# Another order of the pieces, and of every engine's instructions, in an attention and MLP kernel on one core

## The chip, the core and the metric

The kernel runs on one core of a Trainium2 chip. A core has five engines that run beside each other, each with its own list of instructions that it takes in order: TensorE (PE, matmuls; its weight loads are shown as PEld), VectorE (DVE), ScalarE (ACT), GpSimd (POOL, here mostly an issuer of DMAs) and SyncE (SP, an issuer of DMAs). TensorE writes to PSUM, and VectorE and ScalarE take the results from there. Engines wait for each other through semaphores. The metric is the device time of one execution in microseconds; the median of several runs is given.

## What is computed

A recurrent attention over 768 steps for 4 x 8 heads of 40 features, and a two-layer MLP over the 3072 resulting rows.

```python
for t in range(S):
    y[:, :, t] = np.einsum('bhd,bhde->bhe', rt, state)
    Sa = np.einsum('bhde,bhe->bhd', state, at)
    state_decay = state * wt[:, :, None, :] - np.einsum('bhd,bhe->bhde', Sa, bt)
    state = state_decay + np.einsum('bhd,bhe->bhde', vt, kt)
...
h = x @ w_in
sp = np.where(h > 20.0, h, np.log1p(np.exp(np.minimum(h, 20.0))))
g = h * np.tanh(sp)
return (g @ w_out).astype(np.float32)
```

## The kernel before

**Attention.** The 768 steps are cut into 12 chunks of 64. Within a chunk the recurrence is solved with matrices; only a 40 x 40 state per head goes from chunk to chunk. The work is written as small pieces, each named by a letter and by the chunk c and a half (be or g, 0 or 1). Before the state is needed, a chunk goes through: `l` (loads of w, a, b, k by SP), `p` (`scan`, L290 to L305: eight VectorE instructions that make running products of w, each needing the one before but for two), `g` (`gram`, L320: products of a with b and k on TensorE; ScalarE copies them to GP, L321 and L324; VectorE masks a part into HA, L325) and `k` (`natural`, L336 to L351: transposes on TensorE, copied by ScalarE). Two chunks share one inverse of triangular 32 x 32 blocks: `i` (`inverse`, L356 to L368: 65 VectorE instructions, 30 steps of a product L363 and a sum L365, each needing the one before, then the transpose TT, L367, and one more, L368). `m` (`corner`, L377 and L385: 32 x 32 matmuls on TensorE, with copies on ScalarE between), `b` (`blocks`, ScalarE copies, L393) and `t` (`merge`, L404: 64 x 64 matmuls) make of it the chunk's matrix KT.

**State.** For each chunk and half: `V` (ScalarE puts the state beside v, L426), `A` (TensorE, L434, copied to UVT by ScalarE), `T` (transposes of UVT, L442, copied to UVQ by ScalarE, L443), `D` (transposes of the state, L450, copied by ScalarE, L451), `B` (L462 on TensorE into the PSUM tile pq, of which there is one; VectorE masks it into UVQ in two instructions, L465), `C` (L484 and L491 on TensorE, into pq too; VectorE adds the state, L494, and scales it, L498; ScalarE copies the result to yev, L496). The new state lets the next chunk's V, A and D start. `v`, `u`, `q` are POOL's loads of VS, UVT and bdr for the next chunk, `o` its store of a chunk's result.

**MLP.** It works on 6 blocks of 512 rows. `x` loads a block, `X` splits it into a high and a low part. For each of 8 slices of the hidden layer, `h` (`mlp1`, L656: 16 matmuls, then the Mish on ScalarE), `H` (`split_g`: ScalarE rounds, L663, VectorE takes the rest, L664) and `y` (`mlp2`, L677 to L679: 24 matmuls); `z` stores. `w0` to `w3` and `W0` to `W7` load the two weight matrices in chunks and convert them from 64-bit floats: ScalarE scales (L561), VectorE assembles in three instructions (L563 to L565), ScalarE rounds (L584) and VectorE takes the rest (L585). w0 to w3 have three chunks of 128 x 512 each. `+p`, `+i`, `+e` and `/p`, `/i`, `/e` open and close pools of SBUF.

**What sets the order.** Two texts. `SEQ` lists the pieces in the order in which they are built, which decides the turns in which buffers are used. `PLAN` lists for each engine, in order, every instruction of every piece: `g4.0*16` stands for the next 16 instructions of piece g4.0 on that engine. `Lanes.order` turns each such list into a chain in which every instruction comes after the one ahead of it:

```python
for t in plan.split():
    k, n = (t.split('*') + ['1'])[:2]
    for _ in range(int(n)):
        i = next(q[k])
        if last is not None:
            self.tc.add_manual_dep(i, last.name, info, reason='plan')
        last = i
```

So an engine that waits for one instruction holds back all that stand behind it in its list.

Of the kernel before, what the change touches and what calls it, by code (L numbers as in the profile page):

```python
# [48 lines left out]
    D3.1 B3.0 V3.1 T3.0 l7.1 C3.0 g7.0 A3.1 p7.1 v4 D4.0 V4.0 B3.1 T3.1 k7.0 u4 l8.0 C3.1 q4 g7.1 k7.1 b2 p8.0 D4.1 V4.1
    i3 m2.1 l8.1 m2.0 o3 p8.1 t5.0 t4.0 t4.1 t5.1 A4.1 A4.0 B4.1 v5 g8.0 T4.0 B4.0 C4.0 g8.1 T4.1 C4.1 k8.0 u5 V5.0 l9.0  # L50
    k8.1 D5.0 q5 A5.0 V5.1 o4 D5.1 p9.0 T5.0 l9.1 A5.1 B5.0 T5.1 v6 C5.0 p9.1 g9.0 k9.0 B5.1 u6 l10.0 C5.1 q6 g9.1 V6.0
    k9.1 D6.0 b3 i4 l10.1 m3.1 m3.0 p10.0 D6.1 V6.1 t7.1 t6.0 p10.1 t6.1 g10.0 A6.1 A6.0 o5 B6.1 t7.0 v7 T6.0 B6.0 k10.0
    C6.0 T6.1 l11.0 C6.1 u7 p11.0 V7.0 D7.0 q7 A7.0 g10.1 o6 k10.1 T7.0 B7.0 l11.1 g11.0 C7.0 V7.1 p11.1 D7.1 A7.1 k11.0
    v8 B7.1 T7.1 u8 C7.1 q8 g11.1 V8.0 D8.0 k11.1 /p +p w0 i5 b4 m4.0 V8.1 D8.1 m4.1 o7 t8.1 t8.0 w1 t9.0 A8.1 A8.0 B8.1
    v9 T8.1 t9.1 T8.0 B8.0 C8.0 C8.1 u9 V9.0 D9.0 q9 A9.0 D9.1 V9.1 o8 w2 T9.0 A9.1 B9.0 v10 T9.1 b5 m5.0 C9.0 m5.1 B9.1
    C9.1 D10.0 u10 V10.0 t11.0 q10 t10.0 D10.1 o9 V10.1 t10.1 t11.1 /i +i x0 A10.0 A10.1 B10.0 v11 T10.0 T10.1 C10.0 B10.1
    C10.1 V11.0 D11.0 w3 u11 A11.0 X0 q11 D11.1 V11.1 A11.1 o10 h0.0 x1 B11.0 h0.1 H0.0 C11.0 H0.1 h0.3 B11.1 h0.2 X1
    C11.1 /e +e W0 h0.5 H0.2 H0.3 h0.4 o11 H0.5 x2 h0.6 W1 H0.4 h0.7 W2 y0.0 h1.0 X2 y0.1 H0.7 W3 h1.1 H0.6 x3 y0.2 W4
    h1.2 H1.0 h1.3 y0.3 W5 X3 h1.4 H1.1 y0.4 W6 y0.5 h1.5 W7 y0.6 H1.2 H1.3 h1.6 y0.7 z0.0 z0.1 y1.0 H1.4 h1.7 H1.5 z0.2
    z0.3 h2.1 x4 y1.1 H1.6 y1.2 H1.7 y1.3 H2.1 X4 y1.4 y1.5 h2.0 h2.2 H2.0 y1.6 H2.2 y1.7 h2.3 H2.3 h2.4 z1.0 y2.0 z1.1  # L60
    H2.4 h2.5 z1.2 z1.3 h2.7 H2.5 y2.1 h2.6 y2.2 H2.6 H2.7 y2.3 x5 h3.1 y2.4 H3.1 h3.0 X5 H3.0 y2.5 y2.6 y2.7 h3.2 H3.2
    z2.0 z2.1 h3.3 z2.2 y3.0 h3.5 z2.3 H3.3 h3.4 H3.5 H3.4 y3.1 y3.2 h3.6 H3.6 y3.3 h3.7 h4.2 H3.7 h4.0 H4.2 y3.4 H4.0
    h4.1 y3.5 y3.6 H4.1 y3.7 h4.3 h4.4 H4.3 z3.0 z3.1 H4.4 y4.0 h4.6 z3.2 z3.3 y4.1 h4.5 H4.5 y4.2 y4.3 H4.6 h4.7 y4.4
    H4.7 h5.0 h5.1 H5.0 H5.1 h5.2 y4.5 H5.2 y4.6 h5.3 y4.7 H5.3 z4.0 z4.1 y5.0 h5.4 z4.2 z4.3 H5.4 y5.1 y5.2 h5.5 h5.6
    H5.5 h5.7 H5.6 y5.3 H5.7 y5.4 y5.5 y5.6 y5.7 z5.0 z5.1 z5.2 z5.3
# [8 lines left out]
        D3.0*4 C2.1*32 t3.1*32 g6.1*16 A3.0*16 D3.1*4 k6.1*8 B3.0*32 k6.1*4 T3.0*8 k6.1*4 A3.1*16 C3.0*32 g7.0*16 k7.0*8
        D4.0*4 B3.1*32 T3.1*8 C3.1*16 k7.0*4 C3.1*16 g7.1*16 k7.1*8 D4.1*4 k7.1*4 m2.1*32 k7.1*4 m2.0*32 m2.1*32 m2.0*32
        t5.0*32 t4.0*32 t4.1*32 t5.1*32 A4.1*16 g8.0*16 B4.1*32 A4.0*16 g8.1*16 B4.0*32 T4.0*8 k8.0*12 T4.1*4 C4.0*32 T4.1*4
        D5.0*4 C4.1*32 A5.0*16 k8.1*8 D5.1*4 k8.1*4 T5.0*8 A5.1*16 B5.0*32 g9.0*16 k8.1*4 T5.1*4 C5.0*32 T5.1*4 k9.0*8 B5.1*32
        k9.0*4 C5.1*32 g9.1*16 k9.1*8 D6.0*4 k9.1*4 m3.1*32 k9.1*4 m3.0*32 m3.1*32 D6.1*4 m3.0*32 t7.1*32 t6.0*32 t6.1*32
# [720 lines left out]
```

## Time and profile before

| | us |
|---|---|
| median of 3 runs | 754.79 |
| the 3 runs | 750.35, 757.13, 754.79 |
| the profiled execution | 750.2 |
| its span, from the first to the last instruction | 748.3 |
| first MLP matmul starts | 392.94 |
| last MLP matmul ends | 743.39 |

The columns of a group or timeline line are: start or line, duration, engine, line of the kernel, operation, what is written and read, shape and count; in square brackets, how long the engine stood idle before it and what ended that. A wait line gives the total in us, how many waits and the longest. A window line gives the stretch, its length and the busy time of each engine with the number of its instructions, then the granted share of TensorE's clock. TensorE's matmuls overlap, so that a busy TensorE is not one at its peak. In the trace an ordinary 32-bit matmul has two records; a transpose, or a matmul of the MLP, has one.

### The profile page before, as it was taken

Reading aid. Unit: us, or ns where it says so; the run is one execution under the profiler, and the core shown is the slowest. Engines: PE = TensorE matmul, PEld = TensorE weight load, DVE = VectorE, ACT = ScalarE, POOL = GpSimd, SP = SyncE. Lnnn points to the kernel's source line nnn. Section 1 sums busy time; section 2 is a strip of 40 time slices with the busy share of each in tenths; the row PEclk is TensorE's granted clock in tenths of the full one; section 3 lists DMA queues with packets and bytes.
Section 4 is the critical chain, followed back from the end, with each engine's and each line's share of the span. In section 5 each row is a group of like instructions: output and inputs, shape, how many; then the busy total and the mean of one; then the engine's idle time right before and its main releaser. Section 6 shows DMA issues by size and latency. Waiting matters only on the chain.

```text
span 748.3 us, 22996 instructions
## 1 busy us (share of the span) xinstructions
PE 650.5 (87%) x10184; PEld 581.7 (78%) x10184; DVE 451.2 (60%) x901; ACT 356.6 (48%) x571; POOL 104.1 (14%) x181
## 2 busy tenths in 40 slices
PE   2655688699789799687879999999999999999997
...
DVE  8689979979989979979367777421231121111110
...
PEclk9999999879989889879999999999999999999999
...
GB/s 216 106 94 84 82 31 153 117 57 137 151 39 153 139 37 152 63 77 157 86 195 169 161 167 106 3 117 1 1 120 1 0 36 1 10 27 1 35 1 36
DMA packets 31347, 62.11 MB, mean 83 GB/s; under 512 B 6800, under 2 KB 19216, under 8 KB 31248
## 3 DMA queue, kind: packets, MB, share of 16 engines
...
## 4 chain that ended last, share of the span: by engine, by line
PE 65%; DVE 14%; issue 9%; ACT 5%; DMA 4%; POOL 1%; SPq 0%; ACTq 0%; POOLq 0%; DVEq 0%
PE pa L656 24%; PE pu L679 4%; PE pu L678 4%; PE pu L677 4%; PE pq L679 4%; PE pq L677 4%; PE pq L678 4%; PE pa L404 3%; PE pq L484 2%; PE pq L462 2%; PE pa L320 2%; DVE tmp L363 2%; PE pa L385 2%; DVE XL L365 2%; PE pu L434 2%
## 5 line engine op out<-in xcount | busy, mean ns | idle before, releaser
L664 DVE TENSOR_TENSOR gl<-g,gh 128x1024 fp32r<-128x1024 f32 x48 | 58.7, 1225 | 196.4 <-ACT gh L663 196.2
L656 PE MATMUL pa<-xh,w_ih 128*128 128x512 f32 x288 | 112.9, 392 | 0.0
L656 PE MATMUL pa<-xh,w_il 128*128 128x512 f32 x288 | 96.7, 390 | 0.0
L663 ACT CAST gh<-g 128x1024 fp32r<-128x1024 f32 x48 | 50.1, 1047 | 93.6 <-PE pq L678 93.2
L657 ACT ACTIVATE g<-pa 128x1024 f32<-128x1024 f32 x48 | 49.3, 1026 | 75.4 <-PE pa L656 48.5
L656 PE MATMUL pa<-xl,w_ih 128*128 128x512 f32 x192 | 74.9, 390 | 0.0
L320 PE MATMUL pa<-bk,wa 40*64 40x128 f32 x768 | 35.1, 324 | 33.9 <-DVE bk L303 26.7
L656 PEld LDWEIGHTS pa<-xh,w_il 128*128 128x128 f32 x288 | 54.1, 188 | 11.4
L656 PEld LDWEIGHTS pa<-xh,w_ih 128*128 128x128 f32 x288 | 54.1, 188 | 10.5
L363 DVE TENSOR_TENSOR tmp<-XL 128x30 f32<-128x30 f32 (+9 forms) x180 | 58.6, 326 | 1.6
L365 DVE TENSOR_TENSOR XL<-XL,tmp 128x30 f32<-128x30 f32 (+9 forms) x180 | 58.6, 325 | 1.6
L679 PE MATMUL pq<-w_oh,gl 128*128 128x320 f32 x192 | 59.3, 309 | 0.0
L679 PE MATMUL pu<-w_oh,gl 128*128 128x320 f32 x192 | 59.3, 309 | 0.0
L677 PE MATMUL pq<-w_oh,gh 128*128 128x320 f32 x192 | 59.3, 309 | 0.0
L678 PE MATMUL pq<-w_ol,gh 128*128 128x320 f32 x192 | 59.3, 309 | 0.0
L678 PE MATMUL pu<-w_ol,gh 128*128 128x320 f32 x192 | 59.2, 309 | 0.0
L677 PE MATMUL pu<-w_oh,gh 128*128 128x320 f32 x192 | 59.2, 308 | 0.0
L320 PEld LDWEIGHTS pa<-bk,wa 40*64 40x64 f32 x768 | 28.3, 162 | 37.0 <-DVE bk L303 27.3
L305 POOL DMA_DIRECT2D pD<-P x48 | 35.1, 734 | 122.3 <-DVE w L295 85.6
L484 PE MATMUL pq<-UVQ,bkn 128*64 128x104 f32 (+1 forms) x768 | 41.1, 263 | 11.2 <-DVE UVQ L465 5.1
L484 PEld LDWEIGHTS pq<-UVQ,bkn 128*64 128x64 f32 x768 | 36.5, 144 | 15.4 <-issue 6.8
L465 DVE TENSOR_TENSOR UVQ<-pq,cst 128x512 f32<-128x512 f32 x48 | 32.0, 683 | 18.0 <-PE pq L462 17.8
...
## 6 DMA issues: line engine op xcount, KB each, us to landing
...
```

What stands on the lines that cost most here:

```text
L305: PQ.dma_start(out=pD[c, be, :, al].rearrange("e (s t) -> e s t", t=64), in_=P3[al * 64:al * 64 + 40, :, 0:64])
L320: PE.matmul(pt[o, al, s // 2], a[q, s], bk[q, s], start=(s < 2), stop=True, skip_group_check=True)
L363: V.tensor_tensor(out=tv, in0=X[:, i + 1:32, i:i + 1].broadcast_to([128, 31 - i, i]), in1=X[:, i:i + 1, 0:i].broadcast_to([128, 31 - i, i] ...
L365: V.tensor_tensor(out=X[:, i + 1:32, 0:i], in0=X[:, i + 1:32, 0:i], in1=tv, op=ALU.add)
L484: PE.matmul(py[be * 64:be * 64 + 64, al, s, 0:n], BKN[c, be][:, u * 40:u * 40 + 64], UVQ[be][:, u, 0:n], start=(s == 0), stop=(c == 0), sk ...
L656: PE.matmul(pt[:, j], w, x, start=(n == 0), stop=(n == 7), skip_group_check=True)
L657: A.activation(g, pt, AF.Mish)
L663: A.copy(gh, g)
L664: V.tensor_tensor(out=gl, in0=g, in1=gh.bitcast(F32), op=ALU.subtract)
L677: PE.matmul(po[i][k], gh[:, j, t], oh, start=(f == 0), stop=False, skip_group_check=True)
L678: PE.matmul(po[i][k], gh[:, j, t], ol, start=False, stop=False, skip_group_check=True)
L679: PE.matmul(po[i][k], gl[:, j, t], oh, start=False, stop=(f == 15), skip_group_check=True)
```

## The change

`SEQ` and all five lists of `PLAN` are replaced by others with the same pieces and the same number of instructions of each piece on each engine. No function is changed. What differs, list by list:

- VectorE: more inverse steps stand ahead of the first B mask behind each inverse. Where the list alternated p6.0 with i2 and p10.0 with i4, these p now come in one run ahead of the inverse, and the inverse steps in runs of their own (i2*19, i4*20). w2 is converted ahead of w1. B0.1, B2.1 and B11.1 come ahead of their other halves.
- TensorE: the halves of m and the products of g and k are moved around the state's pieces; C9.0 comes ahead of m5.1, B9.1 ahead of D10.0, T10.1 is cut in two around C10.0. In the MLP, h and y are interleaved differently.
- ScalarE: the copies follow what they serve; behind the second inverse, m1 is served between the copies b1.
- POOL: q0 behind v0, q1 ahead of u1, and a few neighbours swapped.
- SP: w2 ahead of w1, with the last third of w1 behind x0.

```diff
 PLAN = {
     'PE': '''
...
-        k11.0*4 g11.1*16 D8.0*4 k11.1*12 m4.0*32 k11.1*4 D8.1*4 m4.0*32 m4.1*64 t8.1*32 t8.0*32 t9.0*32 A8.1*16 A8.0*16
-        B8.1*32 T8.1*8 t9.1*32 T8.0*4 B8.0*32 T8.0*4 C8.0*32 C8.1*32 D9.0*4 A9.0*16 D9.1*4 T9.0*8 A9.1*16 B9.0*32 T9.1*4
-        m5.0*32 m5.1*32 T9.1*4 C9.0*32 m5.0*32 D10.0*4 B9.1*32 m5.1*32 C9.1*32 t11.0*32 t10.0*32 D10.1*4 t10.1*32 t11.1*32
-        A10.0*16 A10.1*16 B10.0*32 T10.0*8 T10.1*8 C10.0*32 B10.1*32 D11.0*4 A11.0*16 C10.1*32 D11.1*4 A11.1*16 h0.0*16
-        B11.0*32 h0.1*16 C11.0*32 h0.3*16 B11.1*32 h0.2*16 C11.1*32 h0.5*16 h0.4*16 h0.6*16 y0.0*6 h0.7*16 y0.0*18 y0.1*12
...
+        g11.1*16 k11.1*8 D8.0*4 k11.1*4 m4.1*32 k11.1*4 m4.0*32 m4.1*32 D8.1*4 m4.0*32 t9.0*32 t8.1*32 t8.0*32 t9.1*32 A8.1*16
+        A8.0*16 B8.1*32 T8.0*8 T8.1*4 B8.0*32 T8.1*4 C8.0*32 C8.1*32 D9.0*4 A9.0*16 D9.1*4 T9.0*8 A9.1*16 B9.0*32 T9.1*8
+        m5.0*32 C9.0*32 m5.1*32 m5.0*32 B9.1*32 D10.0*4 m5.1*32 C9.1*32 t10.0*32 t11.0*32 D10.1*4 t10.1*32 t11.1*32 A10.0*16
+        A10.1*16 B10.0*32 T10.0*8 T10.1*4 C10.0*32 T10.1*4 B10.1*32 D11.0*4 A11.0*16 C10.1*32 D11.1*4 A11.1*16 h0.0*16
+        B11.1*32 h0.1*16 B11.0*32 h0.3*16 C11.0*32 h0.2*16 C11.1*16 h0.4*16 C11.1*16 h0.5*16 h0.6*16 y0.0*12 h0.7*16 y0.0*12
+        h1.0*16 h1.3*16 h1.1*16 y0.1*15 y0.2*3 y0.1*3 y0.2*3 y0.1*6 y0.2*18 y0.3*12 h1.2*16 y0.3*12 h1.4*16 y0.4*24 h1.5*16
...
     'DVE': '''
...
-        i1 i0 i1*2 p4.0 i1 p4.1 i1 p4.1 i1 p4.1 i1 p4.1 i1 p4.1 i1 p4.1 i1 p4.1 i1 p4.1 i1*12 B0.0 i1 B0.0 i1*4 g4.0 i1*2 C0.0
-        i1 C0.0 i1 C1.0 i1*3 B0.1 i1 B0.1 i1*2 p5.0 i1 p5.0 i1 C0.1 i1 C0.1 i1 p5.0 i1 p5.0 i1 p5.0 i1 p5.0 i1 g4.1 p5.0 i1
-        p5.0 B1.0*2 i1 C1.1 i1*5 g5.0 i1 C1.0 i1 p5.1 i1 p5.1 i1 p5.1 i1 p5.1 i1 p5.1 B1.1*2 p5.1 i1 p5.1 i1 p5.1 i1 C1.0 i1
-        C1.1 i1 g5.1 i2 C1.1 i2 C2.0 i2*2 p6.0 i2 C2.1 i2 p6.0 i2 p6.0 i2 p6.0 i2 p6.0 i2 p6.0 i2 p6.0 i2 p6.0 i2 p6.1 i2 p6.1
-        i2 p6.1 i2 p6.1 i2 p6.1 i2 p6.1 i2 p6.1 i2 p6.1 i2*2 B2.0 i2 B2.0 i2*5 g6.0 i2 C2.0 i2 C2.0 i2 C3.0 i2*3 B2.1 i2 B2.1
...
+        p4.0 i1 p4.0 i1 p4.0 i1 p4.1 i1 p4.1 i1 p4.1 i1 p4.1 i1 p4.1 i1 p4.1 i1 p4.1 i1 p4.1 i1*15 B0.1 i1 B0.1 i1*5 B0.0 i1
+        B0.0 i1 g4.0 i1*3 C0.0 i1 C0.0 i1 C1.0 i1*4 C0.1 i1 C0.1 i1 C1.1 p5.0 i1 p5.0 i1 p5.0 i1 p5.0*3 i1 B1.0*2 p5.0 g4.1
+        p5.0 i1*2 C1.0 i1 p5.1 i1 p5.1 i1 p5.1 i1 g5.0 i1 B1.1 i1 B1.1 i1 p5.1 i1 p5.1 i1 p5.1 C1.0 p5.1 C1.1 p5.1 C1.1 p6.0
+        C2.0 p6.0 C2.1 p6.0*6 i2 g5.1 i2*19 p6.1 i2 p6.1 i2 p6.1 i2 p6.1 i2 p6.1 i2 p6.1 i2 p6.1 i2 p6.1 i2 B2.1 i2 B2.1 i2*3
...
+        i3*2 p9.1 i3 p9.1 B5.1*2 p9.1 i3 p9.1*3 C5.1 p9.1 p10.0 p9.1 C5.1 p10.0 C6.1 p10.0*6 i4 g9.1 i4*20 p10.1 i4 p10.1 i4
...
-        C10.1*2 X0*2 w3*7 B11.0*2 H0.0 w3 H0.1 w3*4 B11.1*2 W0 X1 W0*2 X1*2 W0 H0.2 H0.3 W0*3 H0.5 W0 W1*3 H0.4 W1*4 X2 W1
...
+        B9.1*2 C9.1*2 w2 C10.1 w1 B10.0*2 w1*3 C10.0 w1 C10.0 w1*2 B10.1*2 w1 X0 C10.1*2 X0*2 w1*4 w3*3 B11.1*2 H0.0 w3
+        B11.0*2 H0.1 w3*5 X1 w3*2 X1 w3 X1 W0*3 H0.2 H0.3 W0*4 H0.4 W0 W1 H0.5 W1*3 X2 W1 H0.6 W1*2 X2 W1 X2 W2*8 W3*4 H0.7
...
     'Pool': '''
-        z*7 q0 v0 q0 p0.0*2 v0 u0*2 p0.1*2 z*2 k0.0 k0.1 k1.0 k1.1 k2.0 k2.1 k3.0 k3.1 p1.0*2 p1.1*2 p2.0*2 p2.1*2 p3.0*2
-        p3.1*2 p4.0*2 p4.1*2 v1*2 u1*2 q1*2 k4.0 k4.1 o0*2 p5.0*2 v2*2 u2*2 p5.1*2 k5.0 k5.1 q2*2 p6.0*2 o1*2 p6.1*2 v3*2 u3*2
+        z*7 v0 q0 v0 p0.0*2 u0 q0 u0 p0.1*2 z*2 k0.0 k0.1 k1.0 k1.1 k2.0 k2.1 k3.0 k3.1 p1.0*2 p1.1*2 p2.0*2 p2.1*2 p3.0*2
+        p3.1*2 p4.0*2 p4.1*2 v1*2 q1*2 u1*2 k4.0 k4.1 o0*2 p5.0*2 v2*2 p5.1 u2*2 p5.1 k5.0 k5.1 q2*2 p6.0*2 o1*2 p6.1*2 v3*2
...
     'SP': '''
-        l6.1*4 l7.0*4 l7.1*4 l8.0*4 l8.1*4 l9.0*4 l9.1*4 l10.0*4 l10.1*4 l11.0*4 l11.1*4 w1*3 w2*3 x0*12 w3*2 x1*5 w3 x1*5 W0
+        l6.1*4 l7.0*4 l7.1*4 l8.0*4 l8.1*4 l9.0*4 l9.1*4 l10.0*4 l10.1*4 l11.0*4 l11.1*4 w2*3 w1*2 x0*12 w1 w3 x1*5 w3 x1*5 w3
...
```

More of the change, by code (lines that the diff above doesn't have):

```diff
@@ L49 @@
[L49 to L63, printed above, removed]
@@ new lines @@
+    l5.1 C1.0 v2 T1.1 B1.1 p5.1 g5.0 u2 k5.0 C1.1 b1 q2 m1.0 l6.0 m1.1 D2.0 p6.0 D2.1 g5.1 k5.1 V2.1 o1 i2 V2.0 t2.1 l6.1
+    t2.0 p6.1 t3.1 A2.1 A2.0 B2.1 v3 T2.0 g6.0 T2.1 B2.0 C2.0 C2.1 t3.0 u3 k6.0 V3.0 l7.0 D3.0 q3 g6.1 A3.0 V3.1 p7.0 o2
+    D3.1 k6.1 T3.0 B3.0 l7.1 A3.1 v4 T3.1 C3.0 p7.1 g7.0 k7.0 B3.1 u4 C3.1 l8.0 V4.0 g7.1 k7.1 q4 D4.0 D4.1 o3 b2 i3 m2.1
+    l8.1 m2.0 p8.0 V4.1 p8.1 t5.0 t4.0 t4.1 g8.0 A4.1 A4.0 B4.1 v5 T4.0 t5.1 B4.0 C4.0 T4.1 C4.1 k8.0 u5 l9.0 V5.0 A5.0 q5
+    g8.1 p9.0 V5.1 D5.0 o4 T5.0 k8.1 B5.0 C5.0 D5.1 l9.1 A5.1 v6 T5.1 p9.1 g9.0 B5.1 k9.0 u6 b3 C5.1 l10.0 m3.0 q6 m3.1
@@ new lines @@
+    D6.0 V6.0 p10.0 V6.1 D6.1 g9.1 k9.1 o5 i4 t6.1 l10.1 t6.0 p10.1 t7.0 A6.1 A6.0 B6.1 v7 T6.0 t7.1 g10.0 B6.0 C6.0 T6.1
+    C6.1 k10.0 u7 l11.0 V7.0 D7.0 q7 A7.0 g10.1 p11.0 V7.1 o6 D7.1 k10.1 T7.0 B7.0 A7.1 l11.1 v8 C7.0 T7.1 g11.0 p11.1
+    B7.1 k11.0 u8 C7.1 q8 g11.1 V8.0 k11.1 /p +p w0 D8.0 b4 i5 D8.1 m4.1 m4.0 V8.1 o7 t9.0 t8.1 w2 t8.0 t9.1 A8.1 A8.0
+    B8.1 v9 T8.0 T8.1 B8.0 C8.0 C8.1 u9 V9.0 D9.0 q9 A9.0 D9.1 V9.1 w1 o8 T9.0 A9.1 B9.0 v10 T9.1 b5 m5.0 m5.1 C9.0 D10.0
+    B9.1 C9.1 u10 t10.0 V10.0 t11.0 q10 t10.1 D10.1 V10.1 o9 t11.1 /i +i x0 A10.0 A10.1 T10.0 v11 B10.0 C10.0 T10.1 B10.1
@@ new lines @@
+    V11.0 C10.1 D11.0 u11 w3 A11.0 X0 q11 D11.1 V11.1 A11.1 o10 h0.0 x1 B11.1 h0.1 H0.0 B11.0 h0.3 H0.1 C11.0 h0.2 X1
+    C11.1 /e +e W0 h0.4 H0.2 H0.3 h0.5 o11 H0.4 x2 h0.6 W1 H0.5 y0.0 h0.7 W2 h1.0 H0.6 X2 y0.1 h1.3 W3 x3 y0.2 H0.7 W4
+    h1.1 h1.2 H1.0 y0.3 W5 X3 y0.4 H1.1 h1.4 W6 y0.5 H1.3 h1.5 W7 H1.2 y0.6 h1.6 y0.7 H1.4 h1.7 z0.0 h2.0 z0.1 H1.5 x4
+    y1.0 z0.2 h2.1 z0.3 y1.1 H1.6 y1.2 X4 H1.7 y1.3 y1.4 H2.0 H2.1 y1.5 y1.6 y1.7 h2.2 z1.0 h2.3 z1.1 H2.2 y2.0 H2.3 h2.4
+    z1.2 z1.3 H2.4 y2.1 h2.5 y2.2 h2.6 H2.5 H2.6 h2.7 y2.3 H2.7 y2.4 h3.2 x5 y2.5 H3.2 y2.6 h3.1 X5 h3.0 H3.1 H3.0 y2.7
@@ L66 @@
+    h3.3 h3.4 z2.0 z2.1 H3.3 y3.0 z2.2 z2.3 H3.4 h3.5 H3.5 h3.6 h3.7 y3.1 y3.2 H3.6 H3.7 y3.3 y3.4 h4.1 h4.0 H4.1 y3.5
+    H4.0 h4.2 y3.6 H4.2 h4.3 H4.3 y3.7 z3.0 z3.1 y4.0 h4.4 z3.2 z3.3 H4.4 y4.1 h4.5 H4.5 y4.2 h4.6 H4.6 y4.3 h4.7 H4.7
+    h5.0 y4.4 H5.0 y4.5 h5.1 h5.3 H5.1 h5.2 H5.3 y4.6 H5.2 y4.7 z4.0 z4.1 y5.0 h5.4 z4.2 z4.3 H5.4 y5.1 h5.5 H5.5 y5.2
+    h5.6 y5.3 H5.6 y5.4 h5.7 y5.5 H5.7 y5.6 y5.7 z5.0 z5.1 z5.2 z5.3
 '''
@@ L74 @@
[L74 to L78, printed above, removed]
@@ new lines @@
+        A1.1*16 C1.0*32 g5.0*16 k4.1*4 T1.1*4 B1.1*32 T1.1*4 k5.0*12 C1.1*32 m1.0*32 m1.1*32 D2.0*4 m1.0*32 D2.1*4 g5.1*16
+        m1.1*32 k5.1*12 t2.1*32 k5.1*4 t2.0*32 t3.1*32 A2.1*16 A2.0*16 B2.1*32 T2.0*8 g6.0*16 T2.1*8 B2.0*32 t3.0*32 k6.0*8
+        C2.0*32 k6.0*4 C2.1*32 D3.0*4 A3.0*16 g6.1*16 D3.1*4 T3.0*4 k6.1*8 T3.0*4 B3.0*32 k6.1*4 A3.1*16 C3.0*32 k6.1*4 T3.1*4
+        g7.0*16 B3.1*32 T3.1*4 k7.0*8 C3.1*32 k7.0*4 g7.1*16 k7.1*8 D4.0*4 k7.1*4 m2.1*32 k7.1*4 m2.0*32 m2.1*32 D4.1*4
+        m2.0*32 t5.0*32 t4.0*32 t4.1*32 g8.0*16 A4.1*16 A4.0*16 t5.1*32 B4.1*32 T4.0*8 k8.0*8 T4.1*4 B4.0*32 T4.1*4 k8.0*4
```

127 lines of the change are left out of this document (59 added, 68 removed).

## The prediction

> **What bounds the kernel now.** First the slices of the page, which split the run into two halves that have nothing in common.
>
> ```profile
> span 748.3 us, 22996 instructions
> PE 650.5 (87%) x10184; PEld 581.7 (78%) x10184; DVE 451.2 (60%) x901; ACT 356.6 (48%) x571; POOL 104.1 (14%) x181
> ...
> PE   2655688699789799687879999999999999999997
> ...
> DVE  8689979979989979979367777421231121111110
> ...
> PEclk9999999879989889879999999999999999999999
> ```
>
> VectorE stands at 8 or 9 tenths up to slice 19 (about 350 us), TensorE from slice 21 to the end. I then asked for windows cut at the end of the first inverse (its last transpose, L368), at the ends of the second to sixth TT (L367, the transpose of a finished inverse, which TensorE waits for), and at the first and last MLP matmul. Columns: PE, PEld, DVE, ACT, POOL busy, clock, DMA share, GB/s.
>
> ```profile
> 91.28:140.04 48.76, 42.48 (x1174) 38.41 (x1175) 43.23 (x107) 26.68 (x52) 13.00 (x24) 0.97 0.36 94
> 140.04:198.08 58.04, 49.99 (x1408) 44.71 (x1406) 52.65 (x125) 38.49 (x73) 17.25 (x31) 0.88 0.39 103
> 198.08:252.47 54.39, 46.26 (x1388) 41.45 (x1388) 50.99 (x121) 34.68 (x64) 15.72 (x28) 0.94 0.45 117
> 252.47:308.40 55.93, 49.03 (x1392) 43.83 (x1392) 51.31 (x121) 34.80 (x66) 14.85 (x27) 0.88 0.39 103
> 308.40:352.73 44.33, 33.18 (x1012) 29.23 (x1012) 39.76 (x100) 31.45 (x54) 7.08 (x12) 0.85 0.32 90
> 352.73:392.94 40.21, 32.70 (x1125) 29.11 (x1125) 20.97 (x35) 28.73 (x47) 7.40 (x12) 0.96 0.53 149
> 392.94:743.39 350.45, 350.45 (x2180) 317.87 (x2176) 114.49 (x144) 134.09 (x166) 2.00 (x4) 1.00 0.17 51
> ```
>
> From 392.94 to 743.39 TensorE has no idle time, so an order cannot shorten it; 4.9 us of tail (748.3 - 743.4) follow. From 91.28 to 352.73, 261.45 us, VectorE works 237.9 us (91%) and TensorE 220.9 (84%). So the end is set by three pieces: VectorE's list up to the sixth TT, the 40.2 us from there to the first MLP matmul, and 350.45 us that stay. What VectorE waits for in the first piece:
>
> ```profile
> DVE UVQ L465 <- PE pq L462: 13.1, 6, 4.2
> DVE HA L325 <- ACT GP L324: 3.1, 3, 2.3
> DVE cv_w L563 <- ACT cv_d L561: 1.7, 1, 1.7
> DVE w L290 <- DMA wa<-in_wa: 1.6, 3, 0.7
> DVE w_il L585 <- ACT w_ih L584: 0.6, 2, 0.4
> ```
>
> Most is in-order waiting: VectorE stands at B's mask (L465) for TensorE's B (L462) while its own inverse work lies behind that mask in the list.
>
> **The change, part by part.** (a) VectorE's neighbours. What an order costs here is whether an instruction needs the result of the one just before it:
>
> ```profile
> 93.28 1.23 DVE L292 TENSOR_TENSOR_SCAN P<-wa,d 128x520 f32<-128x520 f32 x1
> 94.43 0.22 DVE L363 TENSOR_TENSOR tmp<-XL 128x84 f32<-128x84 f32 x1
> ...
> 100.93 0.37 DVE L363 TENSOR_TENSOR tmp<-XL 128x198 f32<-128x198 f32 x1
> 101.33 0.37 DVE L365 TENSOR_TENSOR XL<-XL,tmp 128x198 f32<-128x198 f32 x1
> ```
>
> The inverse step at 94.43 needs nothing of the scan and starts 0.08 us before the scan's end (94.51). The pair below is dependent and leaves 0.03 us free. Over the whole list the median distance is -0.082 and +0.034 us, so a dependent neighbour costs 0.116 us more. Counting them in the two lists up to the sixth TT (i after i, p after p of one scan): 105 before, 176 after, because runs such as i2*19 and i4*20 replace alternations with p6.0 and p10.0. 71 x 0.116 = +8.2 us on VectorE.
>
> [...]
>
> (b) Work moved over the sixth TT. Before, 11 instructions of w1 stand ahead of it, after, 7 of w2: four instructions less, one 128x512 weight chunk. A chunk is 0.43 + 3 x 0.69 us by the rows at 377.75 below, 0.08 less each when overlapped: -2.1 us. They go where VectorE is busy 20.97 of 40.21 us, so they cost nothing; without that cover, 2.1.
>
> (c) The waits, -16.2 us at stake (13.1 + 3.1). The first:
>
> ```profile
> 90.04 1.24 DVE L368 STREAM_TRANSPOSE GP<-TT 128x1024 f32<-128x1024 f32 x1
> ...
> 107.15 0.69 DVE L465 TENSOR_TENSOR UVQ<-pq,cst 128x512 f32<-128x512 f32 x1 [4.21 <-PE pq L462]
> ```
>
> TensorE delivers the first B 15.9 us after the inverse ended (91.28 to 107.15). VectorE's list has 31 instructions between, 11.8 us of work; the new list has 42, 16.3 us. The wait of 4.2 goes. The later ones likewise, TT to B on TensorE against VectorE's new work in between (durations of the same rows, summed): second inverse 23.2 against 26.7, third 19.4 against 23.1, fourth 25.9 against 32.3. For the fifth 28.1 against 25.6 plus 2.3 of waiting for weights (1.7 + 0.6 above): about level.
>
> Not all goes. From C0.0's state update to B1.0's mask the new list holds 6.4 us of work (12.5 before), and TensorE has C0.1, A1.0, D1.0, g4.1, k4.1, D1.1 and B1.0 to do there, about 7 us by their rows: 1.0 kept. p10.0 is moved ahead of g9.1; 6.0 us after B5.1's mask begins it needs the load l10.0, which follows k9.0, and C5.1 needs TensorE: 1.5 kept. The three waits for GP: 1.0 kept. I take 3.5; the ends are 0 and 16.2. The other waits above (3.9 us) stay.
>
> (d) TensorE. Changes of tile shape up to the first h: 178 before, 193 after. Eight transposes followed by eight of the same shape, against four followed by another:
>
> ```profile
> 108.03 1.09 PE L442 MATMUL pu<-cst,UVT 128*128 128x128 f32 x8
> 108.96 1.04 PE L336 MATMUL pa<-cst,bk 128*128 128x128 f32 x8
> ...
> 121.72 0.66 PE L450 MATMUL pu<-cst,ST 128*128 128x128 f32 x4
> 122.31 1.16 PE L462 MATMUL pq<-bdr,UVT 40*64 40x64 f32 x64
> ```
>
> 0.93 us for eight is 0.116 each; 0.59 for four is 0.12 more than that, the price of a change. 15 x 0.12 = 1.8 us. 14 of the 15 lie before m5, where TensorE has 40 us idle, and cost nothing there; were TensorE the bound, 1.8. After m5 it is one more, 0.1.
>
> The clock:
>
> ```profile
> 145.60:159.25 13.65, 10.63 (x380) 10.19 (x378) 13.58 (x38) 9.82 (x18) 4.09 (x6) 0.50 0.29 80
> ...
> 360.64:364.05 3.41, 1.82 (x102) 1.62 (x96) 0.86 (x2) 1.76 (x4) 0.73 (x1) 1.00 0.00 0
> ...
> 364.05:367.46 3.41, 3.09 (x45) 2.87 (x38) 0.43 (x1) 2.69 (x5) 0.76 (x2) 0.50 0.36 101
> ```
>
> TensorE is halved in stretches that begin at the merge of an inverse. All but the last lie under VectorE's list, so their going is worth nothing beyond (c). The last falls on the 40.2 us:
>
> ```profile
> 355.52 1.65 PE L484 MATMUL pq<-UVQ,bkn 128*64 128x104 f32 x32
> 360.05 1.02 PE L462 MATMUL pq<-bdr,UVT 40*64 40x64 f32 x50
> 362.66 0.46 PE L462 MATMUL pq<-bdr,UVT 40*64 40x64 f32 x14 [1.58 <-issue]
> 364.62 3.01 PE L484 MATMUL pq<-UVQ,bkn 128*64 128x104 f32 x32 [0.32 <-DVE UVQ L465]
> 374.76 0.53 PE L404 MATMUL pa<-T,HA 64*40 64x64 f32 x18 [1.46 <-issue]
> ```
>
> The same 32 products take 3.01 us instead of 1.65: 1.4 us. I leave it in.
>
> [...]
>
> (e) The 40.2 us. C9.0 goes ahead of m5.1, B9.1 ahead of D10.0, and four of T10.1's transposes behind C10.0 (4 x 0.1 = -0.4). The rest is the same work in a line; the stalls named issue (1.58, 1.46) are not set by order as far as I can see. -0.4 + 0.1.
>
> (f) Queues. POOL issues bdr (q1) ahead of UVT (u1), which was late:
>
> ```profile
> 114.60 1.47 POOL L417 DMA_DIRECT2D UVT<-in_vD  x2 [8.39 <-PE pq L462]
> 116.06 1.10 POOL L422 DMA_DIRECT2D bdr<-in_rD  x2
> ...
> 120.52 1.06 PE L442 MATMUL pu<-cst,UVT 128*128 128x128 f32 x8 [0.72 <-DMA UVT<-in_vD]
> ```
>
> 1.1 us later for q1, but its releaser, B0's second half and T0, ends some 6 us sooner: no cost. SP loads w2 before w1, and the last third of w1 now lies behind x0's 12 loads. VectorE's w1*4 and w3*3 stand ahead of B11.1's mask; before it was w3*7, again two chunks loaded behind x0. I take 0; the bound is a chunk that comes late:
>
> ```profile
> 377.75 0.43 DVE L563 TENSOR_SCALAR cv_w<-cv_d 128x512 int32<-128x512 int32 x1 [7.71 <-ACT cv_d L561]
> 378.21 0.69 DVE L564 SCALAR_TENSOR_TENSOR cv_w<-cv_d,cv_w 128x512 int32<-128x512 int32 x1
> ```
>
> up to +7.7. ACT's copies move with what they serve (m1 ahead of b1, for one) and ACT is busy at most 71% of a window (31.45 of 44.33): 0. In the MLP h1.0, h1.3 and h1.1 come before y0.1; there is no idle time to win and a broken chain costs.
>
> Sum: +8.2 - 2.1 - 16.2 + 3.5 - 0.4 + 0.1 = -6.9, say -7.0. The profiled execution took 750.2 us, span 748.3; it becomes 743.2. It lies 4.6 under the median of the three runs, 754.8 (750.4 to 757.1); the median becomes 747.8.
>
> **The rivals.** Slower: the waits move and do not go. In the trace most masks start within 0.1 us of TensorE's B, so the chain C, state, A, B may bind as much as VectorE does. Then (a) and (b) stand alone, 754.8 + 6.1 = 761. It decides once less than 6.1 of the 16.2 us goes. Against it: VectorE's share of 91%.
>
> No effect: the sixth TT comes earlier but the 40.2 us grow by as much, because weights and x0 land when they did: 754.8. For it: VectorE waited 7.7 us for a chunk there; against: no matmul before the first h needs one.
>
> More: also the issue stalls and the half clock of the 40.2 us go (1.6 + 1.5 + 1.4 = 4.5), 747.8 - 4.5 = 743.
>
> Dependent neighbours cost nothing, the early start being bookkeeping: 747.8 - 8.2 = 739.6. [...]
>
> **How the numbers follow.** Forecast 0.54, its own range 742 to 754; slower rival 0.15, no effect 0.13, more 0.13, free neighbours 0.05. A measurement here tells about 1% from no change, so faster means under 747.3 and slower over 762.3. Faster: half of the forecast's share less a little (0.25), the last two rivals (0.18), together 0.43. Slower: about half of that rival, half of late chunks, and a broken MLP chain, 0.14. Same 0.43. The range runs from 739, the free neighbours, to 760, just short of the slower rival.
>
> **What would show it.** In the changed profile: VectorE's waits for pq L462 between the first inverse and the sixth TT near 2 us instead of 13; the sixth TT near 346 instead of 352.7; more dependent gaps in the timeline of i2 and i4; still 40 us to the first h and 350.4 us behind it. The prediction is wrong if new waits of C (L494) or of p (L290) appear, if the 40 us change by several, or if TensorE idles in the MLP.

## The result, and the profile after

The changed kernel takes 749.33 us (median of 20 runs, 744.55 to 754.05), the kernel before, run beside it, 756.3 us (20 runs, 750.35 to 762.12). The ratio is 0.9914, 95% interval 0.9892 to 0.9937: about 0.9% faster. Medians here and below are over all executions, ratios over those in the fast state alone, so a ratio is not the quotient of the two medians. The profiled execution of the changed kernel took 749.9 us.

The page first, then its windows, cut at the same events as in the prediction (end of the first inverse, end of the second to sixth TT, first and last MLP matmul), with the columns given there.

```profile
span 748.1 us, 22984 instructions
...
PE 652.8 (87%) x10184; PEld 583.2 (78%) x10184; DVE 455.8 (61%) x901; ACT 359.2 (48%) x571; POOL 104.9 (14%) x181
...
DVE  7689999799899999999267768521222122111100
...
PEclk9999999779879989979899999999999999999999
```

```profile
90.71:133.60 42.89, 39.47 (x1136) 35.92 (x1140) 41.70 (x106) 24.91 (x48) 12.41 (x22) 1.00 0.35 88
133.60:197.70 64.10, 53.38 (x1428) 47.49 (x1421) 56.18 (x126) 36.72 (x68) 16.78 (x30) 0.81 0.38 99
197.70:249.80 52.10, 44.88 (x1326) 40.52 (x1316) 47.90 (x117) 36.06 (x67) 12.47 (x22) 0.90 0.42 108
249.80:310.80 61.00, 52.18 (x1498) 46.10 (x1496) 58.78 (x130) 37.95 (x71) 19.74 (x36) 0.92 0.43 114
310.80:350.20 39.40, 30.93 (x1009) 27.26 (x1008) 38.22 (x96) 31.19 (x53) 7.00 (x12) 0.87 0.33 97
350.20:392.60 42.40, 35.05 (x1137) 31.12 (x1129) 21.11 (x36) 28.93 (x47) 7.53 (x13) 0.92 0.46 133
392.60:743.20 350.60, 350.60 (x2178) 317.77 (x2176) 116.32 (x148) 135.64 (x168) 2.01 (x4) 1.00 0.17 53
```

The MLP is the same to 0.15 us. The sixth TT comes at 350.20 instead of 352.73, but the 40.21 us behind it have become 42.40, and the first MLP matmul starts only 0.3 us sooner. The second window shows where an early lead goes: the second TT is 6.4 us ahead of before (133.6 against 140.04), and the third only 0.4 (197.70 against 198.08).

VectorE's waits between the end of the first inverse and the sixth TT, and the timeline where the largest of them stands:

```profile
DVE GP L353 <- ACT GP L321: 6.1, 3, 4.9
DVE w L287 <- DMA wa<-in_wa: 2.5, 3, 1.7
DVE UVQ L462 <- PE pq L459: 2.4, 5, 1.3
DVE stn L491 <- PE pq L488: 0.3, 1, 0.3
```

```profile
133.98 1.58 PE L374 MATMUL pa<-TT,GP 32*32 32x32 f32 x88
...
139.50 1.27 PE L374 MATMUL pa<-TT,GP 32*32 32x32 f32 x40 [3.94 <-issue]
...
144.94 2.08 PE L317 MATMUL pa<-bk,wa 40*64 40x128 f32 x32 [0.22 <-ACT T L385]
...
148.14 0.74 ACT L321 COPY GP<-pa 32x256 f32<-32x256 f32 x2
148.91 1.23 DVE L353 TENSOR_TENSOR GP<-GP,cst 128x1024 f32<-128x1024 f32 x1 [4.88 <-ACT GP L321]
```

(The changed text is three lines shorter: L459 here is L462 before, L491 is L494, L353 is L356.) The waits for B, 13.1 us before, are 2.4. In their place VectorE waits 6.1 us for GP, once for 4.88: it stands at the first instruction of i2, which needs g5.1, and g5.1 (L317 at 144.94) stands behind the corner matmuls m1.0 and half of m1.1 on TensorE. In the first half of m1.1, between two records of one series of the same 32 x 32 products, TensorE itself stands still for 3.94 us, and nothing in the trace ends that (`issue`). The sections on a_gp and on the stalls show that the wait of 4.88 is for the most part this stall, handed on.

The stretch behind the sixth TT, TensorE's timeline and VectorE's waits:

```profile
352.84 1.65 PE L481 MATMUL pq<-UVQ,bkn 128*64 128x104 f32 x32
...
360.62 0.48 PE L459 MATMUL pq<-bdr,UVT 40*64 40x64 f32 x4 [1.99 <-issue]
...
363.92 3.04 PE L481 MATMUL pq<-UVQ,bkn 128*64 128x104 f32 x32
...
370.84 0.36 PE L401 MATMUL pa<-T,HA 64*40 64x64 f32 x9 [1.27 <-issue]
```

```profile
DVE cv_w L560 <- ACT cv_d L558: 8.8, 1, 8.8
```

The stretch at half clock is still there (3.04 us for 32 records of a product that take 1.65 elsewhere) and lasts 6.8 us in the granted clock, 3.4 before. VectorE still waits for a chunk, 8.8 us, and no matmul waits for it.

### The profile page after: what moved, and what is told of

The parts are those of the page before. It is cut to its first block, busy times and chain, and to the rows that moved or that the text cites. A ratio compares the mean times of both kernels' runs of the same rounds, so it can differ in the third digit from the quotient of the medians.

```text
span 748.1 us, 22984 instructions
## 1 busy us (share of the span) xinstructions
PE 652.8 (87%) x10184; PEld 583.2 (78%) x10184; DVE 455.8 (61%) x901; ACT 359.2 (48%) x571; POOL 104.9 (14%) x181
## 3 DMA queue, kind: packets, MB, share of 16 engines
q1 hardware_dynamic: 22800, 40.91, 18.3%
## 4 chain that ended last, share of the span: by engine, by line
PE 68%; DVE 15%; ACT 6%; issue 6%; DMA 5%; SPq 0%; DVEq 0%; ACTq 0%
PE pa L653 24%; PE pu L676 4%; PE pu L674 4%; PE pu L675 4%; PE pq L676 4%; PE pq L675 4%; PE pq L674 4%; DMA wa<-in_wa 3%; PE pa L317 3%; PE pq L459 3%; DVE XL L362 3%; PE pq L481 3%; DVE tmp L360 3%; PE pa L401 2%; PE pa L333 2%
## 5 line engine op out<-in xcount | busy, mean ns | idle before, releaser
L317 PE MATMUL pa<-bk,wa 40*64 40x128 f32 x768 | 36.5, 337 | 35.5 <-DMA bk<-in_bk 14.2
L653 PEld LDWEIGHTS pa<-xh,w_il 128*128 128x128 f32 x288 | 54.1, 188 | 11.4
L360 DVE TENSOR_TENSOR tmp<-XL 128x30 f32<-128x30 f32 (+9 forms) x180 | 58.6, 326 | 2.8
L317 PEld LDWEIGHTS pa<-bk,wa 40*64 40x64 f32 x768 | 29.0, 169 | 39.8 <-DVE bk L300 25.9
L481 PEld LDWEIGHTS pq<-UVQ,bkn 128*64 128x64 f32 x768 | 36.4, 143 | 15.7 <-issue 9.1
L653 PEld LDWEIGHTS pa<-xl,w_ih 128*128 128x128 f32 x192 | 36.1, 188 | 6.2
```

Of the source, the lines that this page charges most:

```text
L317: PE.matmul(pt[o, al, s // 2], a[q, s], bk[q, s], start=(s < 2), stop=True, skip_group_check=True)
L360: V.tensor_tensor(out=tv, in0=X[:, i + 1:32, i:i + 1].broadcast_to([128, 31 - i, i]), in1=X[:, i:i + 1, 0:i].broadcast_to([128, 31 - i, i] ...
L481: PE.matmul(py[be * 64:be * 64 + 64, al, s, 0:n], BKN[c, be][:, u * 40:u * 40 + 64], UVQ[be][:, u, 0:n], start=(s == 0), stop=(c == 0), sk ...
L653: PE.matmul(pt[:, j], w, x, start=(n == 0), stop=(n == 7), skip_group_check=True)
```

## Experiments

The profiles of all the runs are compared by the same events. "Stretch" is the time from the end of the first inverse (its last transpose) to the end of the sixth TT, "idle" VectorE's idle time in it, "tail" the time from there to the first MLP matmul, "stalls" the sum of TensorE's idle times over 0.25 us, from the end of the first inverse to the first MLP matmul, that nothing in the trace ends. (In head_a3 one such time, 3.27 us at 247.95, is left out: it ends 0.09 us after VectorE has finished a bk, the operand of such a product.) All in us.

| kernel | profiled time | stretch | idle | tail | stalls |
|---|---|---|---|---|---|
| before | 750.2 | 261.4 | 23.5 | 40.2 | 9.0 |
| again_b (before) | 750.5 | 262.5 | 24.3 | 39.8 | 8.4 |
| again_b2 (before) | 749.3 | 260.6 | 22.6 | 39.7 | 8.8 |
| after | 749.9 | 259.5 | 16.7 | 42.4 | 13.9 |
| again_a (after) | 747.1 | 258.2 | 15.7 | 41.6 | 11.4 |
| fill | 758.1 | 269.3 | 30.9 | 40.7 | 13.5 |
| runs | 758.5 | 266.9 | 21.4 | 42.9 | 7.9 |
| head_a | 757.5 | 269.1 | 29.1 | 40.8 | 11.0 |
| head_b | 751.2 | 259.8 | 18.6 | 44.4 | 11.6 |
| head_a3 | 748.1 | 261.4 | 18.3 | 41.1 | 8.8 |
| a_gp | 745.0 | 255.5 | 13.0 | 42.4 | 8.2 |
| a_gp5 | 745.2 | 255.1 | 12.8 | 43.0 | 9.5 |
| shift_b | 754.1 | 264.3 | 26.0 | 41.1 | 8.3 |
| shift_a | 742.5 | 255.6 | 13.1 | 39.4 | 8.5 |

### The two kernels once more

again_b and again_a are unchanged copies.

> The kernel before, profiled once more, since its first profile was of its fastest execution (750.2 us against a median of 756.3 of 20). Theory A (VectorE's list and its waits for B set the time up to the sixth TT): the five waits for B stand at the same places again, 13.1 us in total within 2, the sixth TT near 353 to 358, and a slower execution has longer waits there. Rival B (TensorE stalls at random in its own list, named issue, at every 127th or so matmul): the waits for B stay but the issue stalls of TensorE, 9.1 us in the first profile, are several us more when the time is more, at the same matmul numbers.

> The changed kernel, profiled once more. In its first profile the sixth TT ended at 350.2 us, one stall of TensorE without a releaser (3.94 us inside m1.0, matmul 1740) was followed by a wait of 4.9 us of VectorE for GP before i2. Theory A: that wait is part of the new order and stands there again, sixth TT at 350 or later. Rival B: the stall is a random one; without it the wait shrinks to 1 us or less and the sixth TT ends near 346.

750.5 and 747.07 us, the kernel before beside them 754.47 (19 runs). What is steady in the pairs of profiles: waits for B of 13.1 and 12.1 us before, 2.4 and 0.7 after; waits of i for GP of 6.1 and 5.0 us after; idle time 7 to 9 us less after; a tail 1.4 to 2.6 us longer. What is not steady is the size of TensorE's stalls: at record number 1740 of TensorE in the changed kernel 3.94 and 2.73 us, and the wait before i2 goes with it, 4.88 and 3.29.

### VectorE's list alone

`fill` keeps the kernel before and moves 34 inverse steps ahead of masks and loads of the same inverse that waited, with the number of dependent neighbours unchanged.

```diff
-        ... p4.1 i1*12 B0.0 i1 B0.0 i1*4 g4.0 i1*2 C0.0
+        ... p4.1 i1*23 B0.0 i1 B0.0 i1 g4.0 i1 C0.0
...
-        ... p6.1 i2*2 B2.0 i2 B2.0 i2*5 g6.0 i2 C2.0
+        ... p6.1 i2*11 B2.0 i2 B2.0 i2 g6.0 i2 C2.0
```

> The kernel before with VectorE's list alone changed: 34 inverse steps are moved ahead of the masks B0.0, B2.0, B4.1, B8.0 and of g10.0, where VectorE waited 4.3, 3.7, 1.5, 1.3 and 2.4 us; they come from runs of the same inverse behind these, so the number of dependent neighbours is the same. Theory A (waits of an in-order list): the waits are filled, up to -13.2 us, some given back: -5 to -11. Rival (the chain from C over the state to the next B binds, so VectorE waits a little later for C or the next B): 0, within 2 us.

755.42 us, ratio 0.9999 (0.9958 to 1.004): no gain. Its waits on VectorE in the stretch, and TensorE at 180 us:

```profile
DVE UVQ L465 <- PE pq L462: 8.6, 6, 2.3
DVE stn L494 <- PE pq L491: 7.2, 5, 3.0
DVE HA L325 <- PE pu L450: 5.0, 1, 5.0
```

```profile
179.78 1.12 PE L320 MATMUL pa<-bk,wa 40*64 40x128 f32 x13 [4.92 <-issue]
...
182.74 1.12 PE L450 MATMUL pu<-cst,ST 128*128 128x128 f32 x4
...
183.86 0.69 DVE L325 TENSOR_TENSOR HA<-pa,cst 128x512 f32<-128x512 f32 x1 [5.03 <-PE pu L450]
```

The waits for B fell from 13.1 to 8.6 and came back at C (7.2 and 1.1 more; 0.3 before). A likely reason is that TensorE and VectorE run in step: in the profile of before 10 of the 18 state updates (L494) start within 0.3 us of the end of the product they read, in this one 13. One such pair, from again_b2:

```profile
115.89 1.65 PE L484 MATMUL pq<-UVQ,bkn 128*64 128x104 f32 x32 [0.20 <-DVE UVQ L465]
...
117.59 0.49 DVE L494 TENSOR_TENSOR stn<-ST,pq 128x320 f32<-128x320 f32 x1
```

The product ends at 117.54 and the update starts at 117.59. Work taken out of the gap between B's mask and C's update then only opens that gap. (The count alone doesn't prove it: in the changed kernel it is 12 of 18, and the waits are gone.) The 5.03 us wait is another thing: it is TensorE's stall of 4.92, passed on one for one. The same place (record number 2627) held 0.6 us in the profile of before and 1.34 in that of again_b:

```profile
175.20 0.66 PE L320 MATMUL pa<-bk,wa 40*64 40x128 f32 x13 [1.34 <-issue]
```

### The price of dependent neighbours

`runs` keeps the kernel before and puts p and i from chunk 5 on into groups of four instead of alternating, 97 dependent neighbours more.

```diff
-        ... i2 p6.0 i2 p6.0 i2 p6.0 i2 p6.0 i2 p6.0 i2 p6.0 i2 p6.0 i2 p6.1
+        ... p6.0 i2*3 C2.1 p6.0*4 i2*4 p6.0*3 p6.1 i2*4 p6.1*4 i2*4
```

> The kernel before with the alternation of p and i from chunk 5 on in groups of four, nothing else moved: 97 dependent neighbours more, at 0.116 us each 11.3 us of VectorE time. Theory A (VectorE bounds this stage and the price is real): +8 to +11 us, the rest going into waits that shrink. Rival (the price is real but lies beside TensorE's chain, or the early start is bookkeeping): under +3 us.

759.89 us, ratio 1.005 (1.0008 to 1.0093). At 0.116 us each, 97 make 11.3 us. VectorE's busy time in the stretch rose from 237.95 to 245.47, by 7.5; 97 times the lost overlap of 0.082 is 8.0, so the price holds. The stretch is 5.4 us longer than in the profile of before and the median 5.4 us; by the ratio it is 3.8. The rest of the 11.3 fell into idle time that was there: a third to a half of what is added to VectorE's list shows.

### Which part carries the gain

Three hybrids of the two orders, in all lists at once: `head_a` has the changed order for the pieces ahead of b1 (the second inverse's blocks) and the old one behind, `head_b` the reverse, `head_a3` the changed order ahead of b3.

```diff
-    V1.1 D1.1 C1.0 p5.1 A1.1 v2 T1.1 l6.0 B1.1 u2 C1.1 p6.0 g5.1 k5.1 V2.0 q2 b1 D2.0 D2.1 i2 m1.0 l6.1 V2.1 p6.1 m1.1 o1
+    l5.1 C1.0 v2 T1.1 B1.1 p5.1 g5.0 u2 k5.0 C1.1 l6.0 p6.0 g5.1 k5.1 V2.0 q2 b1 D2.0 D2.1 i2 m1.0 l6.1 V2.1 p6.1 m1.1 o1
```

(head_a, the line of `SEQ` where the two orders meet.)

> Pieces up to b1 (chunks 0 and 1 and the second inverse) in the changed order on every engine, all behind them in the order before; the same operations. In two profiles of each kernel the second TT ends at 140.0 and 138.5 before and at 133.6 and 132.8 after, and from there to the first h it takes 252.9 and 254.8 before, 259.0 and 257.1 after. Theory H (the gain is made by the order of the state's pieces up to the second inverse, and what follows gives some of it back): ratio to before 0.990 to 0.994, so at least as fast as the whole change (0.991). Rival W (as in fill, time won ahead of an inverse turns into waits behind it; the gain needs the later stages): 0.998 to 1.002.

> The reverse: pieces up to b1 in the order before, all behind them in the changed order. Theory H: the later part of the changed order is worth nothing or costs 2 to 4 us, ratio 1.000 to 1.005. Rival W: the gain lies there, ratio 0.990 to 0.994.

> Pieces up to b3 (chunks 0 to 5, four inverses) in the changed order, the rest in the order before. From the end of the first inverse to the fourth TT: 261.2 and 261.0 us less the 91.2 of the start before, that is 161.2 and 161.0; after 159.1 and 155.4; behind it before 140.5 and 141.3, after 142.8 and 144.4. Theory H: like head_a, ratio 0.990 to 0.995. Rival W: half of the gain, 0.995 to 0.998.

head_a 758.28 us, ratio 1.0008 (0.997 to 1.0047); head_b 749.76, 0.9916 (0.9887 to 0.9945); head_a3 751.96, 0.9945 (0.9909 to 0.9981). The whole gain lies behind b1. head_a shows the early part given away: its second TT is at 131.1 us, 8.9 ahead of before, and its third at 202.6, 4.5 behind, and between them VectorE waits 4.1 us for GP, 4.1 for B, and 4.9 behind a stall of TensorE of 4.37 at record number 2629.

### The new wait taken away

`a_gp` is the changed kernel with g5.1 (and D2.0) moved ahead of m1.1.

```diff
-    l5.1 C1.0 v2 T1.1 B1.1 p5.1 g5.0 u2 k5.0 C1.1 b1 q2 m1.0 l6.0 m1.1 D2.0 p6.0 D2.1 g5.1 k5.1 V2.1 o1 i2 V2.0 t2.1 l6.1
+    l5.1 C1.0 v2 T1.1 B1.1 p5.1 g5.0 u2 k5.0 C1.1 b1 q2 m1.0 D2.0 l6.0 g5.1 D2.1 p6.0 m1.1 k5.1 V2.1 o1 i2 V2.0 t2.1 l6.1
...
-        ... C1.1*32 m1.0*32 m1.1*32 D2.0*4 m1.0*32 D2.1*4 g5.1*16
-        m1.1*32 k5.1*12 ...
+        ... C1.1*32 m1.0*32 D2.0*4 m1.0*32 g5.1*16 D2.1*4 m1.1*64
+        k5.1*12 ...
```

> The changed kernel with g5.1 moved ahead of m1.1 (on TensorE, on ScalarE and in the turns of the PSUM buffers), so that GP is there when VectorE comes to i2; in two profiles VectorE stood there 6.1 and 5.0 us for GP in all. Theory A (VectorE's list sets the time): the wait shrinks to 1 us and the kernel gains about 4 us on the changed one, ratio to before 0.986. Rival (the state's chain binds behind the inverse, as fill has it): the wait goes and comes back at a mask or a sum of the state, ratio as for the changed kernel, 0.991, or more.

> The changed kernel with g5.1 moved ahead of m1.1 on TensorE, ScalarE and in the order of the pieces, the same kernel as a_gp, with more rounds. If the wait of VectorE for GP in the third inverse is what the change lost: 745 to 747 us, a ratio to the kernel before of 0.985 to 0.989, below the changed kernel's 0.9914. If the earlier 745.9 was the luck of four runs: 749 us, 0.991.

745.93 us, ratio 0.9873 (0.9809 to 0.9936), and again 745.94 us, 0.9896 (0.9843 to 0.995), each against the kernel before of its own series (756.86 and 755.08). VectorE's waits in the stretch of a_gp, and its second window:

```profile
DVE w L287 <- DMA wa<-in_wa: 2.6, 4, 0.9
DVE stn L491 <- PE pq L488: 2.0, 2, 1.6
DVE UVQ L462 <- PE pq L459: 1.8, 3, 1.3
DVE GP L353 <- ACT GP L321: 1.3, 1, 1.3
```

```profile
132.60:191.60 59.00, 51.37 (x1452) 45.51 (x1440) 56.26 (x126) 37.39 (x70) 17.10 (x30) 0.88 0.42 109
```

The wait for GP falls from 6.1 to 1.3, the window from 64.1 to 59.0, and the sixth TT comes at 345.3. Both medians are 3.4 us under the changed kernel's, but the intervals of the ratios overlap, so that this version is better than the changed one is not settled.

Nor is it shown that the move of g5.1 did it. The stall at number 1740, which lies ahead of g5.1 in both orders, is missing in a_gp, and two runs of other experiments have it small or not at all with g5.1 left behind m1.1:

| kernel | g5.1 | stall at 1740 | VectorE's wait before i2 |
|---|---|---|---|
| after | behind half of m1.1 | 3.94 | 4.88 |
| again_a | behind half of m1.1 | 2.73 | 3.29 |
| head_a3 | behind half of m1.1 | 0.56 | 0.83 |
| shift_a | behind half of m1.1 | none | 0.83 |
| a_gp | moved | none | none |
| a_gp5 | moved | 1.17 | 0.68 |

In shift_a, described in the next section, the same pieces stand in the same order:

```profile
133.41 2.21 PE L374 MATMUL pa<-TT,GP 32*32 32x32 f32 x128
...
140.32 2.08 PE L317 MATMUL pa<-bk,wa 40*64 40x128 f32 x32 [1.41 <-ACT T L385]
...
144.29 1.23 DVE L353 TENSOR_TENSOR GP<-GP,cst 128x1024 f32<-128x1024 f32 x1 [0.83 <-ACT GP L321]
```

So the place of g5.1 costs about 0.8 us, and the rest of the 4.88 and 3.29 is TensorE's stall, handed on nearly one for one. It is what again_a's expectation has as rival B: without the stall a wait under 1 us and a sixth TT near 346 (345.9 in shift_a). The second window of shift_a (end of the second to end of the third TT) is 58.6 us, its stretch 255.6 and its median 745.04, as good as a_gp's without the move.

### What the stalls belong to

`shift_b` and `shift_a` are the two kernels with 28 short products added on TensorE ahead of the first inverse, which write the same values again.

```diff
-            for b2 in range(2):
+            for b2 in [0, 1] * (8 if c == 2 else 1):
...
-        g2.1*16 k2.1*16
+        g2.1*16 k2.1*44
```

> The kernel before with 28 short products added that write the same values again (TensorE, ahead of the first inverse, at k2.1). They move every later instruction of TensorE 28 matmuls further along in its program and change nothing else; their own time is under 2 us, in a place where VectorE is behind. Theory: the stalls named issue belong to places in the program, one block of about 127 matmuls after the other. Then they stand at the same running numbers as before (2627, 3644, 5164, 7198, 7582, give or take 1), now ahead of other work, and their sizes change with the work around them. Rival: they belong to the work, something in these products or their operands; then they stand 28 later (2655, 3672, 5192, 7226, 7610). Time: within 4 us of the kernel before either way, 756; a large one at 2627 gone would give about 752.

> The changed kernel with the same 28 short products added at k2.1. Theory of places: stalls at the same running numbers as in the changed kernel (1740, 3773, 4535, 5170, 7204, 7459, give or take 1). Rival, the work: 28 later (1768, 3801, 4563, 5198, 7232, 7487). Time within 4 us of the changed kernel, 749.5. If the gain of the change came from where these block ends happen to fall, and not from VectorE's waits, the distance of shift_a to shift_b would be well under the 7 us between the two kernels; if it comes from the waits, it stays at 4 us or more.

> The kernel before once more, for one more profile. Its two profiled executions so far took 750.2 and 750.5 us, while the median of its runs is about 756. TensorE's unexplained stalls (named issue) summed to 9.0 and 8.4 us in them, with 0.6 and 1.3 us at matmul 2627. If the size of these stalls is what spreads the runs: an execution of 754 us or more shows a sum larger than 9 by about what it is longer, with 3 to 5 us of it at matmul 2627 (4.9 and 4.4 us stood there in the two other kernels that share this part), and an execution near 750 shows 8 to 10. Rival: the spread comes from the clock or from loads; then a long execution shows the same stalls of 8 to 9 us and more time at the half clock or more waits for DMA.

The running number, among TensorE's matmul records, of the one behind each stall (those over 0.5 us from the end of the first inverse on); such a 32-bit product has two records (four of L349 stand as x8 in the timeline), so the 28 products are 56 numbers:

```
before   979 2627 3644 3770 5164 6562 7198 7582 7708
shift_b  979 3645 5799 6307 6562 7326 7454 7582
after    1740 3773 4535 4916 5043 5170 7204 7459 7587 7713
shift_a  2249 4408 4535 4662 6440 7204 7587
```

They stand at places in the program and not at the work: 979, 6562 and 7582, or 4535, 7204 and 7587, are the same numbers though 56 records were put in ahead, and none stands 56 later. (The 28 of the two expectations counts products; none stands 28 later either.) The places are about 127 records apart (3770 - 3644 = 126, 7582 - 7454 = 128), and the page's queue `instruction` has as many packets as there are such blocks, 10184 / 80 = 127.3 (10184 are TensorE's matmul records):

```profile
q8 instruction: 80, 1.31, 0.8%
```

From these numbers I estimate that TensorE waits there for the next block of its own program; that it is the fetch, no run shows. The stalls are 0.3 to 4.9 us. 1740 is free in shift_a, and 2627 in shift_b.

Times: shift_b 752.46 us, ratio 0.998 (0.9944 to 1.0016); shift_a 745.04, 0.9875 (0.9819 to 0.993). The distance between the two orders stays, 7.4 us, with the block ends at this one other position, so it isn't made by where they fell in the first two kernels. shift_a is 4.3 us under its kernel, which agrees with the stall of 3.94 and 2.73 gone; shift_b is 2.6 us under its own, though no profile of the kernel before had more than 1.34 at 2627. Both differences lie inside the uncertainty of the ratios. again_b2, 749.3 us with stalls of 8.8, again caught a short execution of the kernel before and so could not tell what makes the longer ones. The granted clock of the unprofiled runs doesn't tell either: beside shift_b the kernel before took 759.36 us at 0.892 and 756.49 at 0.932, but 751.25 at 0.906 and 752.01 at 0.914.

## Why the prediction was right, and where it was not

The time was right: 747.8 forecast, 749.33 measured, within the forecast's own range. The way there was right in part. In the profiles of the two kernels themselves the gain is smaller than forecast, 0.3 us between the two that go with the result and 3.4 between again_b and again_a, where the sum had 7.0; between shift_b and shift_a it is 11.6.

(a) and (b), VectorE's list: forecast +8.2 - 2.1 = +6.1. Busy time in the stretch rose from 237.9 to 242.8 (41.70 + 56.18 + 47.90 + 58.78 + 38.22), by 4.8; the 0.034 us left open behind each of the 71 dependent neighbours, 2.4, lie in idle time. Together 7.2, 1.1 too little in the forecast. The rival of free neighbours is out: runs added 7.5 us of busy time without adding an instruction, about 0.08 for each of its 97 new dependent neighbours. The early start stands in the changed kernel's trace too: between an inverse step and a neighbour of another kind the median distance up to the sixth TT is -0.083 us (395 pairs), between two inverse steps +0.034 (149).

(c), the waits. That those for B go was right: 13.1 became 2.4, forecast near 2. The term that was mis-sized is "GP 1.0 kept": the waits for GP were 6.1 and 5.0. The three of before, at g's mask (L325), are gone, and new ones stand at the first instruction of i (L353). With p6.0 ahead of i2 in one run, VectorE has nothing else in its list when it comes to i2, so whatever delays TensorE ahead of g5.1 delays VectorE as much. I had looked at TensorE's stalls behind the sixth TT alone and put them at nothing in the stretch. There the stall at 1740 was 3.94 and 2.73 us, and the wait before i2 4.88 and 3.29; without the stall it is 0.83 (shift_a, whose other wait for GP, 2.73 before i4, follows a stall of 2.18 at 4662). The waits of the stretch fell from 20.4 to 11.3, by 9.1 us; forecast 12.7. 7.2 - 9.1 = -1.9 is what the stretch shows (261.4 to 259.5), where -6.6 was forecast, and 346 became 350.2. In shift_a, with that stall gone, the stretch is 255.6 and the sixth TT comes at 345.9, close to the forecast, in one profile. C's waits, forecast with 1.5, were 0.3 and 2.5.

The rival of waits that move was wrong for this change and right for fill, which changes VectorE's list alone: no gain. My sentence for it, that masks start within 0.1 us of TensorE's B, was the better reading of the trace (13 of 24 do), and VectorE's share of 91% the weaker one against it. fill's list is not the new one, though, so that TensorE's and ScalarE's new order is what makes VectorE's new list pay is argued and not shown: no run has one without the other.

(d) The half clock (0.50 in the trace) stayed, as I left it in. What sets it off, these traces don't settle: in the profile of before it followed a window in which TensorE was busy for 1.82 of 3.41 us (360.64 to 364.05) and one with 2.94 (200.21 to 203.62), and it did not follow one with 1.83 (340.16 to 343.57). Nor do all its stretches begin at a merge: one began at 135.36, before the second TT. The price of the shape changes was not tried by itself. (e) 40.2 became 42.4 and 41.6, forecast 39.9. Of the 2.2, TensorE's stalls are 0.5 more (1.99 + 1.27 + 0.90 + 0.61 = 4.8, against 1.58 + 0.50 + 1.46 + 0.67 = 4.2 before), and the half clock lasts 3.4 us longer, which costs up to 1.7 (half of 3.4, an estimate). But again_b and shift_a have the same 6.8 us of half clock, and their tails are 39.8 and 39.4, so the clock alone doesn't explain the 2.2; the rest stays open. (f) Nothing came late that a matmul needed, although VectorE's wait for a chunk grew from 7.7 to 8.8. The MLP stayed at 350.6.

The last step, from the profile to the median, held by luck as far as I can tell. I took the profiled execution's distance to the median, 4.6 us, as the same in both kernels. It isn't: the three profiled executions of the kernel before took 749.3 to 750.5, and its medians are 754.5 to 756.9; those of the changed kernel took 747.1 and 749.9, its median is 749.3. So most of the 7 us stands between the profiled and the ordinary executions of the kernel before, and none of the latter was profiled. Two kernels that share its TensorE order behind b1, fill and head_a, were profiled at 758.1 and 757.5, with a stall of 4.9 and 4.4 us at the place that held 0.6 to 1.3 in the short ones, and with stretches of 269 us. It fits that ordinary executions of the kernel before look like these. That the new order has slack where the old one hands such a stall on does not fit: at 1740 the new order handed its own on as well. What makes most of the 7 us was not shown, and it stays open.
